# One-hot rows for the token tables: two values side by side in place of six

## The chip, the cores and the metric

The kernel runs on one core of a Trainium2 chip. The metric is the device time of one execution in microseconds; a kernel is given by the median of its runs. The engines are TensorE (matmuls, PE in the profile; its weight loads PEld), VectorE (DVE), ScalarE (ACT), GpSimd (POOL) and SyncE (SP, which issues most DMAs).

## The reference

Three layers follow each other on 4,608 tokens (8 batches of 576) of 512 features:

```python
# 1. attention without a score matrix, per batch and head (8 heads of 64)
q_s = softmax(q, over the head's features); k_s = softmax(k, over the sequence)
x = q_s @ (k_s.T @ v)                       # (4608, 512)
# 2. mixture of 8 experts, the best two for each token
n = x @ w_gate + log1p(exp(x @ w_noise)) * noise
top2 = the two largest of n; weights = softmax(n[top2])
out[t] += weight * relu(x[t] @ w1[e]) @ w2[e]      # for the two experts e of token t
# 3. soft mixture: 32 slots, 4 for each of 8 experts
logits = x @ phi; d = softmax over tokens; c = softmax over slots
y = c @ experts(d.T @ x)                    # (4608, 512)
```

For layer 2 the kernel has to find out, on the chip, which tokens belong to which expert. That list, the table of tokens by expert, is what the change is about.

## The kernel before, in words

**Stages.** Tokens are taken in four pairs of batches, nine tiles of 128 tokens each. The attention of pairs 0 to 2 and part of pair 3 runs first (the string FIRST lists its steps in order); then the experts begin with ten blocks of two tiles of tokens from pairs 0 and 1, and the rest of the attention (the string MIX) is spread over these blocks. Then come blocks of three tiles, blocks of two tiles, all under conditions on the number of blocks, and at the end the soft mixture (the tail).

**The gate of a part of a pair.** `gate(T0, T1)` (L329) runs twice for each pair of batches, on six tiles and on three. It computes noisy logits, ranks the experts, and gives each chosen (token, expert) a place: the place's row `bf` (0 to 127) and column `af` (0 to 287, 36 columns for each of 8 experts). The table `tab` of 128 rows by 288 columns then has to hold the token's number + 1 at that place. It is built by matmuls: for the tile t and choice q of its tokens, `ob` holds in each token's row a one-hot row of 128 values, scaled by the token's number (L419 compares with the constant columns `k.cols`, L420 multiplies with `k.tok1`), and `oa` a one-hot row of 288 values (L427, in `columns`). The matmul of L437 multiplies the two and sums over all tiles and choices in `pa`: twelve matmuls for six tiles, six for three. L442, or L445 to L447, add `pa` to `tab`.

**Layout before.** All are 2-byte floats. `ob` is laid out as [128 partitions, 128 columns, 12 rows], `oa` as [128 partitions, 288 columns, 6 rows]; the constant `k.cols` repeats each number six times (L85). VectorE works on six rows at a time (CW = 6), so neighbouring values in memory are six rows' values of one column, and a matmul that takes one row reads every twelfth value of `ob` (24 bytes apart) as weights and every sixth of `oa` (12 bytes apart) as the moving operand.

**Order.** The steps are emitted in the order of FIRST and MIX; a gate is a generator that goes on at the entries "bg". Within that, a planner orders each engine's instructions by its own costs. Every engine works its queue in order, so that a matmul waiting for VectorE's rows holds up what stands behind it on TensorE.

**Other lines that the prediction's steps name:** L268 and L269 (k.T @ v), L299 and L303 (attention's output), L277 (scaling k.T @ v on VectorE), L744 (splitting weights into two parts, on ScalarE and VectorE), L762 and L764 (transposing and splitting the experts' rows), L777 (experts' first matmul, 256 columns), L807 (their second, 512 columns), L221 (ScalarE's copy of the maxima).

Of the kernel before, what the change touches and what calls it, by code (L numbers as in the profile page):

```python
# [21 lines left out]
P = 128  # L22
B, H, S, DH = 8, 8, 576, 64
D = H * DH
E = 8
# [6 lines left out]
# blocks of two tiles: NPA on the tokens of the first two pairs of batches, up to NPB later, NST of  # L32
# them in any case; in between up to NTR of three tiles
# [3 lines left out]
GT = 6  # L37
# [4 lines left out]
# steps of attention(): of pair i, part j as "stepi.j", a or v behind it: on ScalarE or VectorE.  # L42
# Those before the experts' first blocks,
# [3 lines left out]
# and during those, spread over SPREAD parts  # L47
# [24 lines left out]
def gate_consts(k, ap):  # L72
    nc = k.nc
    # lt[p', p] = 1 where p' < p
# [6 lines left out]
    # columns 0 .. 287, each CW times  # L81
    it = ap.tile([P, E * TE], I32, name="it")
    nc.gpsimd.iota(it, pattern=[[1, E * TE]], base=0, channel_multiplier=0)
    k.cols = ap.tile([P, E * TE, CW], F16, name="cols")
    nc.scalar.copy(k.cols, it.unsqueeze(2).to_broadcast([P, E * TE, CW]))  # L85
# [4 lines left out]
    # local token number + 1 of (p, j), and E * TE * 128 offsets of experts  # L90
# [10 lines left out]
    # tril[e, f] = 1 where f < e  # L101
    k.tril = ap.tile([P, E, E], F32, name="tril")
    nc.gpsimd.affine_select(out=k.tril, in_=k.ones[:, :64].rearrange("p (e f) -> p e f", e=E), pattern=[[1, E], [-1, E]], compare_op=ALU.is_gt, fill=0.0, base=0, channel_multiplier=0)
    # tri[r, e] = 1 where e < r
# [6 lines left out]
def attention(k):  # L111
    """x rows and the dense gates of every token into k.xtab; the tables of tokens by expert. Pauses
    once when the experts can begin, then after every further step."""
    nc, tc = k.nc, k.tc
    with ExitStack() as ctx:
# [5 lines left out]
        # what the experts take the place of  # L121
# [12 lines left out]
        # columns of two heads in KB, each in its own rows: features, parts of the logits, sums  # L134
# [34 lines left out]
        def zero(n):  # L169
            """Part n of x2, first the rows of the first two pairs; and the rows of x that free places read."""  # L170
            z = zz[n % 2]
            if n < 2:
                nc.gpsimd.memset(z, 0.0)
            # not before the rows of x so far
            nc.gpsimd.tensor_copy(z[:, 0:1], after[0][:, 0:1])
            nc.gpsimd.memset(z[:, 0:1], 0.0)
            if n == NZ:
                nc.sync.dma_start(k.xtab[NTOK:, :D], z)
                nc.sync.dma_start(k.xtab[NTOK:, D:], z[:, :E])
            half = k.x2[:NTOK // 2] if n < NZ else k.x2[NTOK // 2:]  # L180
            xr = half.rearrange("(p r) d -> p r d", p=P)
            n_r = half.shape[0] // P
            r = slice(n % NZ * n_r // NZ, (n % NZ + 1) * n_r // NZ)
            nc.sync.dma_start(xr[:, r], bcast(z, 1, r.stop - r.start))
# [14 lines left out]
        # softmax over the sequence: k - max, exp; the sums come with kv  # L199
# [36 lines left out]
        # softmax over the head's features: q - max, exp; the sums come with x  # L236
# [86 lines left out]
        def heads(T0, T1, eng):  # L323
            """Sums of the heads' parts of the logits."""
            lr = lgrs[T0 // TP][:, T0 % TP:T0 % TP + T1 - T0]
            for w in (4, 2, 1):
                eng.tensor_add(lr[:, :, 0:w], lr[:, :, 0:w], lr[:, :, w:2 * w])

        def gate(T0, T1):  # L329
# [14 lines left out]
            # (w - 1) - u, what 1 + u gained  # L344
# [14 lines left out]
            # rank by value, then by number of expert; the first two are taken  # L359
# [14 lines left out]
            # 7 - e + r1 - r2 of the other seven are before it, under 2 for the two  # L374
# [4 lines left out]
            # place of a token among those of its experts  # L379
# [36 lines left out]
            ob = sp.tile([P, P, 2 * GT], F16, name="ob")  # L416
            parts = [slice(m, m + CW) for m in range(0, 2 * n_t, CW)]
            for ms in parts:
                nc.vector.tensor_tensor(ob[:, :, ms], k.cols[:, :P], bcast(flat(bf)[:, ms], 1, P), op=ALU.is_equal)  # L419
                nc.vector.tensor_tensor(ob[:, :, ms], ob[:, :, ms], bcast(flat(k.tok1)[:, ms], 1, P), op=ALU.mult)  # L420
                yield 1
# [3 lines left out]
            def columns(ms):  # L425
                oas.append(sp.tile([P, E * TE, CW], F16, name="oa", bufs=2))
                nc.vector.tensor_tensor(oas[-1], k.cols, bcast(flat(af)[:, ms], 1, E * TE), op=ALU.is_equal)  # L427
# [6 lines left out]
            for ms in parts:  # L434
                oa = oas.pop(0)
                for m in range(ms.start, ms.stop):
                    nc.tensor.matmul(pa, ob[:, :, m], oa[:, :, m - ms.start], start=m == 0, stop=m == 2 * n_t - 1)  # L437
                if len(oas) and ms.stop < 2 * n_t - CW:
                    columns(slice(ms.stop + CW, ms.stop + 2 * CW))
                yield  # L440
# [10 lines left out]
        def back(n):  # L451
            while bg and n:
                try:
                    # 1 marks where only the last pair's pause
                    if next(bg[0]) is None or fine[0]:
                        n -= 1
                except StopIteration:
                    bg.pop(0)
# [72 lines left out]
def table(k):  # L531
    """Tokens of the tables' places; free ones are given rows of their own."""
    nc = k.nc
    m = k.ac.tile([P, E * TE + TE], F32, name="pl_m")
    nc.vector.memset(m[:, E * TE:], 0.0)
    nc.vector.tensor_scalar(m[:, :E * TE], k.tab, 0.0, k.pad1, op0=ALU.is_equal, op1=ALU.mult)
    nc.vector.scalar_tensor_tensor(m[:, :E * TE], k.tab, -1.0, m[:, :E * TE], op0=ALU.add, op1=ALU.add)
    return m
# [10 lines left out]
def block_experts(k, en, n, eoh, eq):  # L549
    """Experts of n blocks, given the experts' first blocks; and where they are the first of theirs."""  # L550
# [8 lines left out]
def block_loads(k, eq, name):  # L559
    """Experts to load for blocks, E for none."""  # L560
# [12 lines left out]
def plan_first(k, cnt):  # L573
    """The first NPA blocks, of two full tiles each, from the first two pairs of batches."""
# [26 lines left out]
    # how many of each expert these are  # L601
# [4 lines left out]
    # rows of the first block  # L606
# [5 lines left out]
def plan(k, cnt):  # L612
    """The other blocks: of three tiles, one for each expert whose number of tiles is odd, and of two
    tiles; their tokens, experts and numbers."""
# [4 lines left out]
    # tiles of each expert, its pairs and threes; running sums of these  # L619
# [13 lines left out]
    # a three takes a pair, if there is one  # L633
# [11 lines left out]
    # where the tables begin, and where they go  # L645
# [14 lines left out]
    for e in range(E):  # L660
        # an even expert's three is written over
# [6 lines left out]
    # behind the last three is the first pair  # L668
# [24 lines left out]
def experts(k, att, rs):  # L693
    """Blocks of tokens through their experts; the steps of `att` go in between in the first ones."""
    nc, tc = k.nc, k.tc
    with ExitStack() as ctx:
# [3 lines left out]
        # banks by use; there are more of them after the attention  # L700
# [8 lines left out]
        # weights by quarters of the hidden features, then rounded and what that left  # L709
# [9 lines left out]
        # rows of x of the next block, its gates, and the present ones  # L719
# [27 lines left out]
        # numbers of blocks: NPA, NPB and one behind them, NTR of three tiles and one behind them  # L747
# [21 lines left out]
        def hidden(b, u):  # L769
            """Part u of the hidden features of a pair, transposed."""  # L770
# [12 lines left out]
        def hidden1(b, u):  # L783
            """The same of a third tile."""
# [24 lines left out]
        def scatter(b, s, py):  # L809
# [4 lines left out]
            # a pair has free places in its second tile only  # L814
# [4 lines left out]
        def block(b, n_s, n, n_n):  # L819
            """Block b of n_s tiles; what the next block n (of n_n tiles) needs runs ahead."""  # L820
# [3 lines left out]
            # a block that may follow several others finds its first weights in the same buffers  # L824
# [45 lines left out]
        for b in range(NPA):  # L870
            if b == NPA - 1:
                # read by all engines, and by none too early
# [33 lines left out]
        # whatever came last has made the first pair ready  # L906
# [18 lines left out]
# buffers of 8 KB for the tail: NA of weights that are loaded while the experts run, NB and 4 others;  # L925
# where rows, further weights and results go
# [4 lines left out]
def tail_weight(k, n, w, after=None):  # L931
    """Weights of the slots' experts in the order in which they are used: four experts at a time,
    a quarter of the inner dimension at a time, two experts in a buffer. Not loaded before `after` is there."""
# [16 lines left out]
def tail(k, rs, rg):  # L950
    nc, tc = k.nc, k.tc
    with ExitStack() as ctx:
# [30 lines left out]
        # st[(g, s), (h, s')] = 1 where s == s'  # L983
# [33 lines left out]
        # softmax over the tokens of part g of the rows, and its share of the slots' inputs, in steps  # L1017
# [65 lines left out]
        def s_s(g):  # L1083
            """The parts' shares, scaled once all maxima are there; their sum."""
# [8 lines left out]
            # the slots' inputs, transposed, but for the sums' reciprocals; those of other experts' slots are zero  # L1093
# [4 lines left out]
        def s_M(g):  # L1098
            """What the parts' shares are scaled by."""
# [13 lines left out]
        def s_Q(g):  # L1113
            """The reciprocals of the sums, by rows (h, s)."""
# [8 lines left out]
        # softmax over the slots  # L1123
# [36 lines left out]
        def c_tr(i):  # L1160
            """The softmax's rows transposed (hi, lo, hi, lo)."""
# [68 lines left out]
        # the slots' experts  # L1230
# [36 lines left out]
        # the slots' outputs (hi, hi, lo, lo)  # L1267
# [42 lines left out]
def _tiles(a):  # L1310
    """(8, 576, c) -> (4, 128, 9, c): pair of batches, partition, tile."""
# [7 lines left out]
def _untile(t):  # L1319
    """(4608, c) in order of tiles -> (4608, c) in order of batches."""  # L1320
# [32 lines left out]
```

## Time and profile before

| | |
|---|---|
| median of 3 runs | 1271.38 us (1265.96 to 1276.61) |
| profiled execution, first to last instruction (span) | 1266.1 us; what lies around the span is not shown |
| TensorE busy | 1169.8 us, 92% of the span |
| VectorE busy | 821.4 us, 65% |
| ScalarE busy | 586.9 us, 46% |
| GpSimd busy | 371.7 us, 29% |
| instructions | 21,319 |
| granted TensorE clock, mean | 0.962 of full |

Busy shares are averages over stages with different limits: the attention ends at about 215 us, the ten blocks and the blocks of three tiles at about 654, the pairs at 1113, then the tail. The duration of a matmul runs from its start to its modelled end and overlaps with the next one's; how long the engine is held is read from one start to the next.

### The profile page before, as it was taken

Reading aid. Unit: us, or ns where it says so; the run is one execution under the profiler, and the core shown is the slowest. Engines: PE = TensorE matmul, PEld = TensorE weight load, DVE = VectorE, ACT = ScalarE, POOL = GpSimd, SP = SyncE. Lnnn points to the kernel's source line nnn. Section 1 sums busy time; section 2 is a strip of 40 time slices with the busy share of each in tenths; the row PEclk is TensorE's granted clock in tenths of the full one; section 3 lists DMA queues with packets and bytes.
Section 4 is the critical chain, followed back from the end, with each engine's and each line's share of the span. In section 5 each row is a group of like instructions: output and inputs, shape, how many; then the busy total and the mean of one; then the engine's idle time right before and its main releaser. Section 6 shows DMA issues by size and latency. Waiting matters only on the chain. (4 is left out here: it accounts for less than half of the span.)

```text
span 1266.1 us, 21319 instructions
## 1 busy us (share of the span) xinstructions
PE 1169.8 (92%) x7792; PEld 1006.6 (80%) x7792; DVE 821.4 (65%) x1468; ACT 586.9 (46%) x887; POOL 371.7 (29%) x397
## 2 busy tenths in 40 slices
PE   4686789999999999999997999999999999987995
PEld 3675667899789889999886989989889899875642
DVE  7988976758686665555554666666666666664753
ACT  3554564556444454444443544544445445433424
POOL 6655643223334222222123223223232122120000
PEclk9877888999999999999998999999999999998998
DMA  9848235467364566665656838365646336128697
GB/s 342 286 149 286 101 115 179 118 200 242 76 167 107 137 172 170 168 167 150 152 161 177 269 84 219 103 204 109 204 100 159 95 72 164 34 47 301 226 377 303
DMA packets 115336, 218.01 MB, mean 172 GB/s; under 512 B 13712, under 2 KB 53776, under 8 KB 111120
## 3 DMA queue, kind: packets, MB, share of 16 engines
q1 hardware_dynamic: 98176, 176.05, 40.7%
q0 software_dynamic: 17040, 40.44, 17.2%
q8 instruction: 65, 1.06, 0.4%
q14 instruction: 55, 0.45, 0.1%
HBM read 243.31 MB, written 48.65 MB: 231 GB/s over the span
## 5 line engine op out<-in xcount | busy, mean ns | idle before, releaser
L744 DVE TENSOR_TENSOR R1l<-ringS,R1h 128x1024 fp32r<-128x1024 f32 x96 | 117.6, 1225 | 101.7 <-ACT R1h L744 98.3
L744 DVE TENSOR_TENSOR R0l<-ringS,R0h 128x1024 fp32r<-128x1024 f32 x95 | 116.4, 1225 | 102.3 <-ACT R0h L744 95.6
L744 DVE TENSOR_TENSOR R2l<-ringS,R2h 128x1024 fp32r<-128x1024 f32 x91 | 111.5, 1225 | 90.3 <-ACT R2h L744 81.1
L744 ACT ACTIVATE R1h<-ringS 128x1024 fp32r<-128x1024 f32 x96 | 101.7, 1060 | 141.5 <-PE py L807 84.1
L744 ACT ACTIVATE R0h<-ringS 128x1024 fp32r<-128x1024 f32 x95 | 100.8, 1062 | 136.6 <-PE py L807 75.9
L744 ACT ACTIVATE R2h<-ringS 128x1024 fp32r<-128x1024 f32 x91 | 96.5, 1060 | 145.6 <-PE py L807 81.8
L777 PE MATMUL ph<-xh,R0h 128*128 128x256 f32 x400 | 112.6, 282 | 1.1 <-DVEq L898 1.0
L777 PE MATMUL ph<-xl,R0h 128*128 128x256 f32 x400 | 112.9, 282 | 0.0
L690 POOL DMA_INDIRECT xg<-xtab,pl_idx x40 | 49.4, 1234 | 214.3 <-DVE sc L767 199.3
L777 PE MATMUL ph<-xh,R0l 128*128 128x256 f32 x400 | 112.2, 280 | 0.0
L781 DVE SCALAR_TENSOR_TENSOR hl<-ph,hh 128x512 fp32r<-128x512 f32 x140 | 95.8, 685 | 24.0 <-ACT hh L780 20.4
L777 PE MATMUL ph<-xh,R2h 128*128 128x256 f32 x360 | 102.5, 285 | 1.9 <-DVE hl L781 1.9
L777 PE MATMUL ph<-xl,R2h 128*128 128x256 f32 x360 | 102.0, 283 | 0.5 <-DVE xl L764 0.5
L777 PE MATMUL ph<-xh,R2l 128*128 128x256 f32 x360 | 101.8, 283 | 0.0
L777 PE MATMUL ph<-xh,R1h 128*128 128x256 f32 x360 | 101.4, 282 | 0.2 <-DVE hl L781 0.2
L813 POOL DMA_INDIRECT x<-y,pl_idx x40 | 63.6, 1589 | 128.9 <-DVE y L812 118.9
L777 PE MATMUL ph<-xl,R1h 128*128 128x256 f32 x360 | 100.6, 279 | 0.0
L777 PE MATMUL ph<-xh,R1l 128*128 128x256 f32 x360 | 100.5, 279 | 0.0
L780 ACT ACTIVATE hh<-ph 128x512 fp32r<-128x512 f32 x140 | 81.8, 584 | 32.5 <-PE ph L777 29.2
L807 PE MATMUL py<-R1l,hh 128*128 128x512 f32 x200 | 80.4, 402 | 0.0
L807 PE MATMUL py<-R1h,hl 128*128 128x512 f32 x200 | 79.3, 398 | 0.0
L777 PEld LDWEIGHTS ph<-xh,R0h 128*128 128x128 f32 x400 | 75.4, 189 | 2.3 <-issue 1.4
(440 smaller groups left out, 3158.9 us busy)
## 6 DMA issues: line engine op xcount, KB each, us to landing
ringS<-in_moe_w_dram SPq DMA_DIRECT2D x292, 512.0 KB
ringA<-in_moe_w_dram SPq DMA_DIRECT2D x12, 1024.0 KB
ringA<-in_moe_w_dram SPq DMA_DIRECT2D x22, 512.0 KB
xtab<-xr SPq DMA_DIRECT2D x36, 256.0 KB
kt<-in_k_dram SPq DMA_DIRECT2D x8, 1024.0 KB
v<-in_v_dram SPq DMA_DIRECT2D x8, 1024.0 KB
x<-z SPq DMA_DIRECT2D x5, 1280.0 KB
ringS<-x SPq DMA_DIRECT2D x5, 1024.0 KB
```

The lines of the kernel that those rows point to most:

```text
L690: k.nc.gpsimd.indirect_dma_start(out=x, out_offset=None, in_=k.xtab[:n], in_offset=bass.IndirectOffsetOnAxis(ap=idx, axis=0))
L744: turn[1:] = [nc.scalar.activation(r[0], f, AF.Copy), nc.vector.tensor_sub(r[1], f, r[0].bitcast(F32))]
L777: nc.tensor.matmul(ph[:, g, :], w[i][:, c, g * P:(g + 1) * P], x[:, c, :], start=n == 0, stop=n == 11)
L780: nc.scalar.activation(hh[:, fs, :], ph, AF.Relu)
L781: nc.vector.scalar_tensor_tensor(hl[:, fs, :], ph, 0.0, hh[:, fs, :].bitcast(F32), op0=ALU.max, op1=ALU.subtract)
L807: nc.tensor.matmul(py[s], a[h], w[i][:, f, :], start=u == 4 and f == n == 0, stop=u == 7 and f == 1 and n == 2)
L813: d = nc.gpsimd.indirect_dma_start(out=k.x2[:NTOK // 2] if b < NPA else k.x2, out_offset=bass.IndirectOffsetOnAxis(ap=at(b, s), axis=0), i ...
```

## The change

`k.cols` repeats each column number twice in place of six times. `ob` is laid out as [128 partitions, tile, 128 columns, 2 choices] and `oa` as [128 partitions, 3 tiles, 288 columns, 2 choices], so that the two choices of one tile's token lie side by side, and a matmul reads every second value (4 bytes apart). VectorE still handles three tiles (six rows) in one instruction; constant columns and the values compared are broadcast to that shape. Comments are taken out elsewhere in the file; that is left out here.

```diff
-    k.cols = ap.tile([P, E * TE, CW], F16, name="cols")
-    nc.scalar.copy(k.cols, it.unsqueeze(2).to_broadcast([P, E * TE, CW]))
+    k.cols = ap.tile([P, E * TE, 2], F16, name="cols")
+    nc.scalar.copy(k.cols, it.unsqueeze(2).to_broadcast([P, E * TE, 2]))
...
-            ob = sp.tile([P, P, 2 * GT], F16, name="ob")
-            parts = [slice(m, m + CW) for m in range(0, 2 * n_t, CW)]
+            ob = sp.tile([P, GT, P, 2], F16, name="ob")
+            parts = [slice(m, m + CW // 2) for m in range(0, n_t, CW // 2)]
+            over = lambda x, ms, n: bcast(x[:, ms], 2, n)
             for ms in parts:
-                nc.vector.tensor_tensor(ob[:, :, ms], k.cols[:, :P], bcast(flat(bf)[:, ms], 1, P), op=ALU.is_equal)
-                nc.vector.tensor_tensor(ob[:, :, ms], ob[:, :, ms], bcast(flat(k.tok1)[:, ms], 1, P), op=ALU.mult)
+                n_p = ms.stop - ms.start
+                nc.vector.tensor_tensor(ob[:, ms], bcast(k.cols[:, :P], 1, n_p), over(bf, ms, P), op=ALU.is_equal)
+                nc.vector.tensor_tensor(ob[:, ms], ob[:, ms], over(k.tok1, ms, P), op=ALU.mult)
                 yield 1
...
             def columns(ms):
-                oas.append(sp.tile([P, E * TE, CW], F16, name="oa", bufs=2))
-                nc.vector.tensor_tensor(oas[-1], k.cols, bcast(flat(af)[:, ms], 1, E * TE), op=ALU.is_equal)
+                n_p = ms.stop - ms.start
+                oas.append(sp.tile([P, CW // 2, E * TE, 2], F16, name="oa", bufs=2)[:, :n_p])
+                nc.vector.tensor_tensor(oas[-1], bcast(k.cols, 1, n_p), over(af, ms, E * TE), op=ALU.is_equal)
...
-                for m in range(ms.start, ms.stop):
-                    nc.tensor.matmul(pa, ob[:, :, m], oa[:, :, m - ms.start], start=m == 0, stop=m == 2 * n_t - 1)
-                if len(oas) and ms.stop < 2 * n_t - CW:
-                    columns(slice(ms.stop + CW, ms.stop + 2 * CW))
+                for m in range(2 * ms.start, 2 * ms.stop):
+                    nc.tensor.matmul(pa, ob[:, m // 2, :, m % 2], oa[:, m // 2 - ms.start, :, m % 2], start=m == 0, stop=m == 2 * n_t - 1)
+                if len(oas) and ms.stop < n_t - CW // 2:
+                    columns(slice(ms.stop + CW // 2, ms.stop + CW))
                 yield
```

## Rows read from the trace of the kernel before

**Rows 1.** Busy us by stage: window, length, PE, PEld, DVE, ACT, POOL, clock, DMA.

```profile
100.00:140.00 40.00, 32.48 (x194) 27.07 (x194) 35.86 (x88) 24.67 (x46) 22.62 (x27) 0.82 0.70 230
...
215.40:654.00 438.60, 435.77 (x2832) 389.87 (x2831) 271.94 (x502) 205.24 (x307) 117.00 (x123) 0.99 0.57 154
...
676.00:1113.00 437.00, 432.46 (x2799) 391.23 (x2800) 276.43 (x390) 209.32 (x257) 117.42 (x103) 0.99 0.52 138
```

**Rows 2.** The tiles ob, oa, cols: count, ns min/median/max, first and last start.

```profile
L437 PEld LDWEIGHTS <-ob x72: 138/145/168, 100.7 to 363.5; 128*128 128x128 f16 x72
L437 PE MATMUL pk<-oa,ob x72: 544/567/587, 100.7 to 363.9; 128*128 128x288 f16 x72
L419 DVE TENSOR_TENSOR ob<-cols,bf x12: 546/557/2699, 93.5 to 353.9; 128x768 f16<-128x768 f16 x12
...
L427 DVE TENSOR_TENSOR oa<-cols,af x12: 1008/1051/1142, 91.5 to 352.9; 128x1728 f16<-128x1728 f16 x12
...
L85 ACT CAST cols<-it x1: 1631/1631/1631, 2.1 to 2.1; 128x1728 f16<-128x1728 int32 x1
```

**Rows 3.** TensorE in order of time: start, us, instructions [idle before <-releaser].

```profile
100.69 4.84 PE L437 MATMUL pk<-oa,ob 128*128 128x288 f16 x12 [7.19 <-DVE ob L420]
...
140.58 2.51 PE L437 MATMUL pk<-oa,ob 128*128 128x288 f16 x6 [1.14 <-DVE ob L420]
...
155.57 1.09 PE L283 MATMUL pt<-ident,KB 128*128 128x128 f32 x4 [4.27 <-DVE KB L277]
...
170.56 4.83 PE L437 MATMUL pk<-oa,ob 128*128 128x288 f16 x12
175.22 2.39 PE L299 MATMUL pv<-KB,qT 128*128 128x162 f32 x16
...
183.19 2.47 PE L437 MATMUL pk<-oa,ob 128*128 128x288 f16 x6
...
210.11 4.80 PE L437 MATMUL pk<-oa,ob 128*128 128x288 f16 x12
...
215.42 0.56 PE L777 MATMUL ph<-xh,R1h 128*128 128x256 f32 x1
...
318.72 4.84 PE L437 MATMUL pk<-oa,ob 128*128 128x288 f16 x12
...
323.79 0.63 PE L807 MATMUL py<-R1h,hl 128*128 128x512 f32 x1
324.22 0.63 PE L807 MATMUL py<-R1l,hh 128*128 128x512 f32 x1
```

**Rows 4.** TensorE in order of time, two neighbours of the experts' first matmul.

```profile
219.08 0.28 PE L777 MATMUL ph<-xh,R2l 128*128 128x256 f32 x1
219.20 0.28 PE L777 MATMUL ph<-xh,R2h 128*128 128x256 f32 x1
```

**Rows 5.** Busy us in short stretches; the clock is the number behind POOL.

```profile
100.70:105.40 4.70, 4.70 (x13) 2.00 (x14) 2.10 (x7) 3.65 (x5) 0.00 (x0) 0.50 1.02 293
...
324.00:325.00 1.00, 1.00 (x3) 0.78 (x3) 1.00 (x5) 0.00 (x0) 0.00 (x0) 0.50 0.00 0
...
326.00:327.00 1.00, 1.00 (x8) 0.86 (x7) 0.00 (x0) 0.21 (x1) 0.79 (x2) 1.00 0.62 236
```

**Rows 6.** VectorE in order of time, around three groups of L437.

```profile
94.61 6.50 DVE L420 TENSOR_TENSOR ob<-ob,tok 128x768 f16<-128x768 f16 x2
...
105.56 0.46 DVE L442 COPY tab<-pk 128x288 f32<-128x288 f32 x1 [2.72 <-PE pk L437]
...
175.43 0.46 DVE L445 TENSOR_SCALAR tt<-pk 128x288 f32<-128x288 f32 x1 [5.24 <-PE pk L437]
...
212.04 0.69 DVE L764 TENSOR_TENSOR xl<-ph,xh 128x512 fp32r<-128x512 f32 x1
```

**Rows 7.** One of the page's costliest groups: busy us, mean ns, idle before it.

```profile
L744 DVE TENSOR_TENSOR R1l<-ringS,R1h 128x1024 fp32r<-128x1024 f32 x96 | 117.6, 1225 | 101.7 <-ACT R1h L744 98.3
```

**Rows 8.** ScalarE in order of time, its first work behind L85.

```profile
12.17 0.59 ACT L221 COPY ms<-pt 128x512 f32<-128x512 f32 x1 [8.43 <-PE pt L219]
```

## The prediction

> **What bounds the kernel now.** I read the busy shares by stage first. TensorE is busy 435.8 of 438.6 us between 215.4 and 654 us and 432.5 of 437 us in the later pairs; from 100 to 140 us VectorE is busy 35.9 of 40 us and TensorE 32.5 [rows 1]. So there are two regimes: up to about 215 us a chain that passes between VectorE and TensorE, from there on TensorE alone. Time taken from TensorE's queue counts in full in the second; in the first it counts where VectorE waits for it.
>
> Second, the lines that the change touches. The 72 matmuls of L437 last 567 ns each, their weight loads 145; the VectorE rows take 557 ns (L419, and L420 alike) and 1,051 ns (L427) [rows 2]. Third, TensorE in order of time: how long the queue is held per matmul is read from start to next start, since durations overlap. The twelve from 170.56 hold it until 175.22 [rows 3]: 4.66/12 = 0.388, written 0.389 below, the rate of the other groups too. There are twelve and six for each of four pairs of batches, 72 in all; the sixes of pairs 2 and 3 repeat the one of 183.19. The weight load of 145 ns fits into 0.389, so the moving operand, 288 columns with 12 bytes from one to the next, sets the rate.
>
> The nearest full-rate row is L777: 256 columns of 4-byte values side by side, one matmul every 0.12 us (219.08 to 219.20) [rows 4]. Scaled to 288 columns that is 0.133 us. At the lower clock L807 takes 0.43 us for 512 columns (323.79 to 324.22) [rows 3], so 288 columns would take 0.24.
>
> Fourth, the clock. [...] The engine had been busy with strided matmuls just before it fell. Fifth, who waits: VectorE stands still 2.72 us before L442 at 105.56 and 5.24 us before L445 at 175.43, both for L437 [rows 6].
>
> **The change, part by part.** *The matmuls.* Columns of both operands come to lie 4 bytes apart. No row shows a matmul of 2-byte values at a 4-byte step. Bounds: 0.389 us (nothing gained, the 12-byte step) and 0.133 (4-byte values at a 4-byte step, the same addresses per column). I take 0.133, as the address step equals that of the second row; the gain is 0.256 us a matmul at the full clock, 0.389 - 0.242 = 0.147 at the half.
> [...] No run here shows the new step yet.
>
> Experts' stage (TensorE bound, everything counts):
> - pair 2, six matmuls: 6 x 0.256 = 1.5 us;
> - pair 3, twelve from 318.72: 12 x 0.256 = 3.1, and the half clock behind them: six L807 start in that stretch, at 0.43 in place of 0.24 (twice 256 columns), 1.1 us;
> - pair 3, six matmuls: 1.5.
> Together 7.2 us, 6.1 if the clock still falls.
>
> Attention stage, group by group:
> - pair 0, twelve from 100.69: the engine starts them after 7.19 us of idling and runs at the half clock, so 12 x 0.147 = 1.8 if it stays low, 3.1 if it rises; VectorE can profit by its 2.72 us of waiting at most. I take 2.2.
> - pair 0, six at 140.58: TensorE gains 0.9 to 1.5 us, but then idles 4.27 us for VectorE's L277 at 155.57 [rows 3]; worth 0.
> - pair 1, twelve at 170.56: VectorE's 5.24 us end earlier; 1.8 to 3.1, I take 2.4.
> - pair 1, six at 183.19: between them and L777 at 215.42 TensorE has only short waits, on copies that follow its own work; 1.5, none if the experts' first rows or weights come last.
> - pair 2, twelve at 210.11: L777 behind them starts at 215.42 although its other input, L764's second xl, is there at 212.73 [rows 6]; 1.8 to 3.1, I take 2.4.
> Together 8.5 us, from 5.3 (the low ends, none for the six) to 10.4 (the high ends).
>
> *VectorE's rows.* The same 36 instructions with the same number of elements; the results lie closed up now, but the broadcast operand has runs of two values in place of six. Before, 768 elements in 557 ns and 1,728 in 1,051 ns differ by 960 elements in 494 ns, 0.51 ns an element. No row has runs of two. Bounds: below, nothing (the element rate is the same, and a gap in the output cost nothing that the slope shows); above, the rate of the 4-byte L744, 1,225 ns for 1,024 elements [rows 7], about 1.04 ns an element: +0.41 us for each of 24 and +0.92 for each of 12, 20.7 us of VectorE, of which pairs 0 and 1 and the twelve of pair 2 (12 x 0.92 x 2/3 + 24 x 0.41 x 2/3 = 13.9 us) lie on the chain before 215 us; the rest is hidden under TensorE, VectorE being 272 of 438.6 us busy there [rows 1]. I take nothing: the runs stay closed 4-byte words.
>
> *The constant.* L85 writes 576 values in place of 1,728; it took 1,631 ns [rows 2], and ScalarE has nothing until 12.17 us behind it [rows 8]. Worth nothing; without that cover it would gain about 1 us. No DMA, wait or queue entry is added or moved by hand. The planner orders VectorE's and TensorE's instructions from its own costs, so neighbours may trade places.
>
> **Sum:** 7.2 + 8.5 = 15.7 us, between 11.4 and 17.6. Set against the profiled execution it gives 1266.1 - 15.7 = 1250.4; that span is 0.1 us above the fastest of the three runs and 5.3 under their median, and what lies around it isn't shown. I forecast a median of such runs, so the sum is taken from the median shown: 1271.4 - 15.7 = **1255.7 us**.
>
> **Rivals.**
> 1. *The columns' step isn't the cause, or 4 bytes are still too far for 2-byte values.* Then the pitch stays near 0.389 and the time near 1271. For it: no row has this step. Against: 288 columns at the half clock would need only 0.24, and the rate is the same 0.39 at either clock, so something other than the array holds it. A halfway case (pitch 0.24) would give about 9 us, 1262. Chance 0.12 with the halfway case.
> 2. *VectorE takes runs of two at the 4-byte rate of 1.04 ns an element.* 15.7 gained, up to 13.9 lost: about 1269 to 1270. [...] Against: runs of six show no cost against the 0.51 ns slope. Chance 0.12.
> [...]
> 3. *A wait takes the place of the time saved (slower).* TensorE's queue is in order. In the first group it stood 7.19 us for L420, two instructions of 0.56 us that took 6.50 us from 94.61 [rows 6] while GpSimd worked. If the planner, with other layouts, puts the short matmuls sooner behind their rows, TensorE and all behind it meet such a wait in other groups. At 7.2 us each it decides from the third on: 3 x 7.2 - 15.7 = +6, about 1277. Against: only this group shows a long one (1.14 us at 140.58). Chance 0.08.
> 4. *The gain is there, but the attention stage gives none of it on*, as inputs or GpSimd become the bound: only 7.2 us, 1264. Against: VectorE's two waits. Chance 0.13.
>
> The forecast (11 to 18 us off) keeps 0.55. Its own range is 1254 to 1260, widened by about 5 us either way for the spread of the runs shown. For 8 in 10 the range reaches to rival 4, the halfway case and most of the spread: **1246 to 1268**. One per cent, 12.7 us, is about what a measurement of this kernel can tell from no change. Faster by more takes a gain above 12.7: most of the forecast's share, 0.48, and 0.04 from a halfway case with lucky spread, 0.52. Within one per cent: the rest of the forecast and most of rivals 1, 2 and 4, 0.41. Slower by more: rival 3 and hardly anything else, 0.07.
>
> **What would show it.** L437's starts 0.13 to 0.15 us apart at a granted clock of 1.00 (0.24 at 0.50); L419, L420 and L427 still at 557 and 1,051 ns (958 and 1,958 would be rival 2); VectorE's waits before L442 and L445 shorter by 2 to 3 us; L777's first start near 207 instead of 215.4; no stretch of 0.50 behind pair 3's twelve; everything from the blocks of three tiles on of the same length, only earlier. The prediction fails if the pitch stays, if VectorE's instructions grow, or if a new wait of TensorE appears before 215 us.

## The result and the profile after

The changed kernel takes **1254.3 us** (median of 4 runs, 1252.5 to 1256.1) against 1270.4 us before (4 runs, the three shown above and one more; 1266.0 to 1276.6): a ratio of 0.986 [0.982, 0.990]. That is 16.1 us less; forecast were 15.7 less and 1255.7 us. The profiled execution took 1253.2 us, its span is 1251.3, so 1.9 us lie around the span; its span is 14.8 us shorter than that of before.

The tiles of the change, in the columns of [rows 2]; the lines have moved (L437 is L441 now, L419 L422, L420 L423, L427 L431), L85 has not:

```profile
L441 PEld LDWEIGHTS <-ob x72: 96/97/151, 100.1 to 347.8; 128*128 128x128 f16 x72
L441 PE MATMUL pk<-oa,ob x72: 287/288/448, 100.1 to 347.9; 128*128 128x288 f16 x72
L422 DVE TENSOR_TENSOR ob<-cols,bf x12: 544/548/6207, 92.7 to 339.3; 128x768 f16<-128x768 f16 x12
L423 DVE TENSOR_TENSOR ob<-ob,tok x12: 541/548/1751, 99.5 to 342.2; 128x768 f16<-128x768 f16 x12
...
L431 DVE TENSOR_TENSOR oa<-cols,af x12: 1005/1050/1056, 90.8 to 338.3; 128x1728 f16<-128x1728 f16 x12
...
L85 ACT CAST cols<-it x1: 671/671/671, 2.1 to 2.1; 128x576 f16<-128x576 int32 x1
```

The matmul lasts half as long (288 ns for 567); VectorE's rows have not moved (548 and 1,050 ns for 557 and 1,051). Over the whole span TensorE has 18.3 us less to do (1151.5 for 1169.8). By the pitches below, 60 matmuls that are 0.26 us shorter and 12 that are 0.15 shorter make 17.4 of it; the rest, 0.9 us, is about what other matmuls save that no longer run at the half clock (six at 0.24 in place of 0.43 us are 1.1):

```profile
PE 1151.5 (92%) x7792; PEld 1001.5 (80%) x7792; DVE 821.3 (66%) x1468; ACT 585.5 (47%) x887; POOL 371.0 (30%) x397
```

TensorE in order of time, as in [rows 3]; the experts' first matmul, L777 before, is L781, their second, L807, is L811:

```profile
100.12 3.06 PE L441 MATMUL pk<-oa,ob 128*128 128x288 f16 x12 [7.88 <-DVE ob L423]
102.97 2.19 PE L299 MATMUL pv<-KB,qT 128*128 128x162 f32 x8
...
138.10 0.94 PE L441 MATMUL pk<-oa,ob 128*128 128x288 f16 x6 [0.51 <-DVE ob L423]
...
153.05 1.09 PE L283 MATMUL pt<-ident,KB 128*128 128x128 f32 x4 [6.53 <-DVE KB L277]
...
168.01 2.49 PE L441 MATMUL pk<-oa,ob 128*128 128x288 f16 x12
170.34 2.37 PE L299 MATMUL pv<-KB,qT 128*128 128x162 f32 x16
...
178.28 0.92 PE L441 MATMUL pk<-oa,ob 128*128 128x288 f16 x6
180.01 1.32 PE L303 MATMUL pv<-KB,qT 128*64 128x162 f32 x16 [0.81 <-ACT xr L315]
...
204.52 1.70 PE L441 MATMUL pk<-oa,ob 128*128 128x288 f16 x12
206.05 0.60 PE L256 MATMUL pt<-ident,qt 128*128 128x128 f32 x4
206.53 0.39 PE L781 MATMUL ph<-xh,R1h 128*128 128x256 f32 x1
207.21 0.39 PE L781 MATMUL ph<-xl,R1h 128*128 128x256 f32 x1 [0.29 <-DVE xl L768]
...
308.36 1.70 PE L441 MATMUL pk<-oa,ob 128*128 128x288 f16 x12
309.80 0.49 PE L811 MATMUL py<-R1l,hh 128*128 128x512 f32 x1
...
347.28 0.94 PE L441 MATMUL pk<-oa,ob 128*128 128x288 f16 x6
347.96 0.38 PE L781 MATMUL ph<-xh,R1h 128*128 128x256 f32 x1
```

Twelve matmuls at the full clock now last 1.70 us from the first start to the last end. Less the last one's 0.288 and over eleven steps that is a pitch (the time from one start to the next) of 0.128 us; at the half clock (100.12) it is (3.06 - 0.448)/11 = 0.237.

The clock, in the columns of [rows 5], and the experts' stage, in those of [rows 1]:

```profile
206.50:640.00 433.50, 430.22 (x2841) 388.79 (x2840) 275.08 (x511) 205.36 (x308) 117.92 (x125) 1.00 0.57 156
100.12:102.97 2.85, 2.85 (x12) 1.80 (x13) 2.10 (x7) 2.16 (x4) 0.00 (x0) 0.50 1.00 287
309.80:312.80 3.00, 3.00 (x18) 2.52 (x16) 2.13 (x7) 0.60 (x1) 1.30 (x2) 1.00 0.64 212
206.05:206.70 0.65, 0.65 (x7) 0.54 (x5) 0.65 (x4) 0.00 (x0) 0.00 (x0) 1.00 0.00 0
```

The first group still runs at 0.50. Behind the twelve of pair 3 the clock now stays at 1.00, where it was 0.50 [rows 5]. TensorE is as full as before in the experts' stage (430.2 of 433.5 us). The last row is the stretch behind the twelve of pair 2. In the kernel before, the same stretch, and the six of 183.19 with what follows it, show:

```profile
214.80:215.50 0.70, 0.70 (x6) 0.70 (x4) 0.55 (x2) 0.00 (x0) 0.00 (x0) 0.50 0.00 0
183.20:185.50 2.30, 2.30 (x8) 0.70 (x5) 2.03 (x14) 2.28 (x10) 0.60 (x2) 1.00 0.11 42
185.60:187.60 2.00, 2.00 (x23) 1.77 (x23) 2.00 (x12) 1.00 (x3) 0.00 (x0) 1.00 0.70 262
```

VectorE in order of time, for [rows 6] (L442 is L446, L445 is L449):

```profile
92.73 6.68 DVE L422 TENSOR_TENSOR ob<-cols,bf 128x768 f16<-128x768 f16 x2
...
103.21 0.46 DVE L446 COPY tab<-pk 128x288 f32<-128x288 f32 x1 [0.95 <-PE pk L441]
...
170.54 0.46 DVE L449 TENSOR_SCALAR tt<-pk 128x288 f32<-128x288 f32 x1 [2.90 <-PE pk L441]
```

Its two waits have lost 1.77 and 2.34 us.

**Where the time came from.** The lead of the new kernel over the old one, at the same instruction of both traces, in us:

| instruction (before, after) | lead | step |
|---|---|---|
| first twelve (100.69, 100.12) | 0.6 | 0.6, not from the matmuls |
| L299 behind it (105.35, 102.97) | 2.4 | +1.8 |
| L283 behind pair 0's six (155.57, 153.05) | 2.5 | +0.1 |
| L299 behind pair 1's twelve (175.22, 170.34) | 4.9 | +2.4 |
| behind pair 1's six (185.59, 180.01) | 5.6 | +0.7 |
| experts' first matmul (215.42, 206.53) | 8.9 | +3.3 |
| behind pair 2's six (252.15, 241.80) | 10.4 | +1.5 |
| behind pair 3's twelve (326.50, 311.87) | 14.6 | +4.3 |
| behind pair 3's six (364.38, 348.17) | 16.2 | +1.6 |
| end of the pairs' blocks, the start of the DMA x<-y,pl_idx on the chain that ends last (1113.19, 1097.30) | 15.9 | -0.3 |
| end (1266.1, 1251.3) | 14.8 | -1.1 |

The 0.6 us ahead of the first group is no gain of the change: two other executions of the same changed kernel (after_again and after_5, below) start that group at 102.38 and 100.50. The last 1.1 us are given back in the tail, which has none of the changed work, and are no effect of the change either: from the DMA to the end it takes 154.0 us here and 152.9 before, but 152.9 and 153.6 in those two executions. In them the experts' first matmul starts at 206.82 and 205.61, and the lead at the end of the pairs' blocks is 15.4 and 17.3. So the total lead is good to 1 or 2 us, and the single steps are those of one pair of traces.

### The profile page after: what moved, and what is told of

It reads as the page before. It is cut to its first block, busy times and chain, and to the rows that moved or that the text cites. A ratio compares the mean times of both kernels' runs of the same rounds, so it can differ in the third digit from the quotient of the medians.

```text
span 1251.3 us, 21319 instructions
## 1 busy us (share of the span) xinstructions
PE 1151.5 (92%) x7792; PEld 1001.5 (80%) x7792; DVE 821.3 (66%) x1468; ACT 585.5 (47%) x887; POOL 371.0 (30%) x397
## 5 line engine op out<-in xcount | busy, mean ns | idle before, releaser
L781 PE MATMUL ph<-xh,R0h 128*128 128x256 f32 x400 | 112.6, 282 | 1.1 <-DVEq L902 1.0
L781 PE MATMUL ph<-xl,R0h 128*128 128x256 f32 x400 | 112.6, 282 | 0.0
L781 PE MATMUL ph<-xh,R0l 128*128 128x256 f32 x400 | 112.2, 280 | 0.0
L781 PE MATMUL ph<-xh,R2h 128*128 128x256 f32 x360 | 102.2, 284 | 1.9 <-DVE hl L785 1.9
L781 PE MATMUL ph<-xl,R2h 128*128 128x256 f32 x360 | 102.0, 283 | 0.5 <-DVE xl L768 0.5
L781 PE MATMUL ph<-xh,R2l 128*128 128x256 f32 x360 | 101.8, 283 | 0.0
L781 PE MATMUL ph<-xh,R1h 128*128 128x256 f32 x360 | 100.8, 280 | 0.2 <-DVE hl L785 0.2
L781 PE MATMUL ph<-xl,R1h 128*128 128x256 f32 x360 | 100.4, 279 | 0.3 <-DVE xl L768 0.3
L781 PE MATMUL ph<-xh,R1l 128*128 128x256 f32 x360 | 100.3, 279 | 0.0
L811 PE MATMUL py<-R1l,hh 128*128 128x512 f32 x200 | 79.5, 398 | 0.0
L811 PE MATMUL py<-R1h,hl 128*128 128x512 f32 x200 | 78.8, 396 | 0.0
L781 PEld LDWEIGHTS ph<-xh,R0h 128*128 128x128 f32 x400 | 75.4, 189 | 2.3 <-issue 1.4
```

What stands on the lines that cost most here:

```text
L781: nc.tensor.matmul(ph[:, g, :], w[i][:, c, g * P:(g + 1) * P], x[:, c, :], start=n == 0, stop=n == 11)
L811: nc.tensor.matmul(py[s], a[h], w[i][:, f, :], start=u == 4 and f == n == 0, stop=u == 7 and f == 1 and n == 2)
```

## The experiments

Theory: the moving operand's step sets the matmul's pitch, and all of the gain comes from `oa`. Rivals: `ob`'s step counts too; the attention stage passes nothing on; VectorE pays for its shape. Each kernel is compared with the kernel before on the same chip; edits are against the changed kernel, with lines left out at "...". moving_only, weights_only and late_only also get a second constant that repeats each number six times, for the old half; ScalarE writes it behind L85, in an instruction of the shape of the old L85 (1.63 us in the kernel before), ahead of its other work.

**moving_only** keeps the old `ob` and has the new `oa`.

```diff
-            ob = sp.tile([P, GT, P, 2], F16, name="ob")
+            ob = sp.tile([P, P, 2 * GT], F16, name="ob")
...
-    nc.tensor.matmul(pa, ob[:, m // 2, :, m % 2], oa[:, m // 2 - ms.start, :, m % 2], ...)
+    nc.tensor.matmul(pa, ob[:, :, m], oa[:, m // 2 - ms.start, :, m % 2], ...)
```

> Only the moving operand oa has the new layout (4 bytes from column to column); the weights ob stay 24 bytes apart. Theory (the moving operand's step sets the rate): matmul starts 0.13 to 0.15 us apart at the full clock, the whole gain, 1254 to 1256 us against 1270 before. Rival (the weights' step holds it too): starts 0.25 us apart or more, 1260 or above.

Measured: 1257.8 us, ratio 0.988 [0.981, 0.994], span 1254.5. The tile ob in its trace:

```profile
L444 PEld LDWEIGHTS <-ob x72: 138/143/169, 102.3 to 349.1; 128*128 128x128 f16 x72
L444 PE MATMUL pk<-oa,ob x72: 287/295/459, 102.3 to 349.2; 128*128 128x288 f16 x72
```

Its twelve of pair 3, and the clock behind them:

```profile
309.49 1.80 PE L444 MATMUL pk<-oa,ob 128*128 128x288 f16 x12
```

```profile
311.00:314.00 3.00, 3.00 (x18) 2.52 (x17) 2.11 (x6) 0.60 (x1) 1.21 (x2) 1.00 0.62 197
```

The weight loads are the long ones of before, and the matmuls are short all the same. The loads do show a little: the pitch is (1.80 - 0.295)/11 = 0.137 us for 0.128 in the changed kernel, at loads of 143 ns, which are now longer than the time from one matmul's start to the next. That is 0.6 us over 72 matmuls, which the times can't tell from nothing.

**weights_only** is the other half: the new `ob`, the old `oa`.

```diff
-    oas.append(sp.tile([P, CW // 2, E * TE, 2], F16, name="oa", bufs=2)[:, :n_p])
+    oas.append(sp.tile([P, E * TE, CW], F16, name="oa", bufs=2))
...
-    nc.tensor.matmul(pa, ob[:, m // 2, :, m % 2], oa[:, m // 2 - ms.start, :, m % 2], ...)
+    nc.tensor.matmul(pa, ob[:, m // 2, :, m % 2], oa[:, :, m - 2 * ms.start], ...)
```

> Only the weights ob have the new layout; the moving operand oa stays 12 bytes from column to column. Theory: starts 0.39 us apart as before, weight loads 97 ns in place of 145, and no gain: 1268 to 1272 us. Rival (the weights' step sets the rate): 1254 to 1258.

Measured: 1271.9 us, ratio 1.001 [0.998, 1.004], span 1269.9. Its tile ob, and a stretch behind pair 3's twelve:

```profile
L444 PEld LDWEIGHTS <-ob x72: 96/118/152, 104.6 to 366.9; 128*128 128x128 f16 x72
L444 PE MATMUL pk<-oa,ob x72: 539/562/568, 104.6 to 367.3; 128*128 128x288 f16 x72
```

```profile
327.00:328.00 1.00, 1.00 (x4) 0.77 (x3) 1.00 (x5) 0.00 (x0) 0.00 (x0) 0.50 0.00 0
```

Shorter weight loads are worth nothing beside the slow matmuls (118 ns in the median, against 562 for the matmul). The two halves together show that the gain is `oa`'s, and that the half clock behind pair 3's twelve comes and goes with the slow matmuls (0.50 here, 1.00 in moving_only).

**late_only** has the new layout for pairs 2 and 3 alone (`new = T0 >= 2 * TP`, and the old shapes and matmul where it is false).

> The new layout for the gates of pairs 2 and 3 only; pairs 0 and 1 keep the old one. Theory (what the attention stage gains is passed on to the end): 1.8 + 2.3 + 0.7 = 4.8 us of the changed kernel's gain are lost, 1259 us, and the experts' first matmul starts at about 211 us. Rival (the attention stage's gain is another thing, such as the moment at which the clock rises, and is there anyway): 1254 to 1256, first matmul near 207.

Measured: 1258.4 us, ratio 0.987 [0.982, 0.993], span 1256.4, 5.1 us over that of the changed kernel. Its TensorE at the end of the attention (the experts' first matmul is L797 here):

```profile
209.84 2.17 PE L457 MATMUL pk<-oa,ob 128*128 128x288 f16 x12
...
212.19 0.37 PE L797 MATMUL ph<-xh,R1h 128*128 128x256 f32 x1
```

It reaches the experts 5.7 us after the changed kernel (5.4 and 6.6 after its two other executions) and 3.2 before the old one, so what pairs 0 and 1 save does reach the experts, and nearly all of it the end of the span. The medians stand 4.1 us apart, 2.6 from after_5 on the same chip, with overlapping ranges, so this reading rests on the traces, three of the changed kernel and one of late_only.

**flat_rows** puts the columns side by side (a step of 2 bytes). VectorE's broadcast operand then repeats a single value along the innermost axis, and with it goes the run of two.

```diff
-            ob = sp.tile([P, GT, P, 2], F16, name="ob")
+            ob = sp.tile([P, 2 * GT, P], F16, name="ob")
+            one = lambda x, rs, n: bcast(flat(x)[:, rs], 2, n)
...
-    oas.append(sp.tile([P, CW // 2, E * TE, 2], F16, name="oa", bufs=2)[:, :n_p])
-    nc.vector.tensor_tensor(oas[-1], bcast(k.cols, 1, n_p), over(af, ms, E * TE), op=ALU.is_equal)
+    oas.append(sp.tile([P, CW, E * TE], F16, name="oa", bufs=2))
+    nc.vector.tensor_tensor(oas[-1], bcast(k.cols, 1, 2 * n_p), one(af, rs, E * TE), op=ALU.is_equal)
```

> One-hot rows with the columns side by side (2 bytes apart), so that VectorE's broadcast operand repeats one value in its innermost run. Theory: matmuls no faster than in the changed kernel (0.13 us apart), VectorE's instructions at one element a cycle (958 and 1,958 ns), of which up to 13.9 us lie on the chain before the experts: about 1268 us. Rival (VectorE is covered there): not over 1259. Third: VectorE keeps 550 and 1,050 ns and the time is that of the changed kernel, 1254.

Measured: 1282.0 us, ratio 1.008 [1.004, 1.012], span 1279.3: slower than the kernel before, and 14 us over what was expected. The tiles, then VectorE and TensorE in time:

```profile
L444 PEld LDWEIGHTS <-ob x72: 95/98/152, 105.9 to 365.6; 128*128 128x128 f16 x72
...
L424 DVE TENSOR_TENSOR ob<-cols,bf x12: 895/947/2036, 102.2 to 357.3; 128x768 f16<-128x768 f16 x12
...
L434 DVE TENSOR_TENSOR oa<-cols,af x12: 1943/1952/7611, 92.8 to 355.5; 128x1728 f16<-128x1728 f16 x12
```

```profile
92.85 9.48 DVE L434 TENSOR_TENSOR oa<-cols,af 128x1728 f16<-128x1728 f16 x2
```

```profile
226.83 0.36 PE L784 MATMUL ph<-xh,R1h 128*128 128x256 f32 x1
...
336.99 1.64 PE L444 MATMUL pk<-oa,ob 128*128 128x288 f16 x12
```

The matmuls are as fast as at 4 bytes ((1.64 - 0.286)/11 = 0.123 us), so closing the step wholly gives next to nothing. VectorE takes 947 and 1,952 ns, about twice the time, one element in 1.05 ns ((1,952 - 947)/960) for 0.52 with the run of two. (The expectation's "one element a cycle" is 958 and 1,958 ns worked out from the 1.04 ns an element of L744 [rows 7]; how long a cycle of VectorE lasts no run shows.) The two L434 lost another 5.6 us (9.48 for 2 x 1.95) while GpSimd was at work (94.32 to 100.5). The experts begin 20.3 us later than in the changed kernel, where 13.9 were counted, and pair 3's twelve start 28.6 us later (336.99 against 308.36). The sum left out such standing and the waits that TensorE then has: its L444 matmuls wait 15.9 us for L425's rows, in five places, for 8.4 in two in the changed kernel. The order of the steps is another one too (pair 2's twelve now stand behind the experts' first matmul, from 227.46 on), and how much of the 28 us that accounts for was not separated.
Between these two layouts lie 548 ns with the run of two and 947 with the repeated value, for 768 elements; why the repeated value costs that much no run shows.

**step8** and **step16** keep all of the change but `oa`, whose columns lie 8 and 16 bytes apart. In step8 VectorE takes four rows in an instruction, in step16 six of eight places.

```diff
-NZ, CW = 4, 6
+NZ, CW = 4, 4                       # step8 alone
...
+    oas.append(sp.tile([P, E * TE, 4], F16, name="oa", bufs=2))    # step16: 8 in place of 4
+    o = oas[-1][:, :, 0:2 * n_p].rearrange("p c (t q) -> p c t q", q=2)
+    nc.vector.tensor_tensor(o, bcast(k.cols, 2, n_p), bcast(af[:, ms], 1, E * TE), op=ALU.is_equal)
```

> The moving operand with 8 bytes from column to column (rows of two tiles side by side in fours); the weights as in the changed kernel. VectorE writes oa in five instructions for each pair of batches in place of three. [...] Rival (the rate falls in proportion to the step): 0.24 to 0.26 us apart, 1260 to 1264.

> The moving operand with 16 bytes from column to column (rows of six in places for eight); the weights as in the changed kernel. [...] Rival (any step past 8 bytes costs the same): 0.39 us, 1268 to 1272.

Measured: step8 1269.5 us, ratio 0.998 [0.995, 1.001]; step16 1279.8 us, ratio 1.006 [1.003, 1.010]. A six of step8, with the L813 on either side of it 0.24 us apart as at a clock of 1.00 (0.43 at 0.50), and a twelve of step16, behind which the clock was 0.50 (340 to 343 us):

```profile
322.60 1.70 PE L443 MATMUL pk<-oa,ob 128*128 128x288 f16 x6
```

```profile
334.36 6.26 PE L443 MATMUL pk<-oa,ob 128*128 128x288 f16 x12
```

Their matmuls last 0.436 and 0.687 us in the median; with that taken off for the last one the pitch is (1.70 - 0.436)/5 = 0.253 and (6.26 - 0.687)/11 = 0.507 us; a six of step16 (196.77, 3.21 us) gives 0.505. That 8 bytes would cost no more than 4 (0.13 us apart, 1255 to 1258 us) had been expected, and fell; the rival, that the time goes with the distance, holds from 4 bytes on. For step16 0.389 x 4/3 = 0.52 us and 1276 to 1280 us had been expected, and came; its rival (0.39) fell. The pitches by step:

| step | pitch, us (288 columns) | bytes passed per ns |
|---|---|---|
| 2 bytes (flat_rows) | 0.123 | 4.7 |
| 4 (after) | 0.128 | 9.0 |
| 8 (step8) | 0.253 | 9.1 |
| 12 (before) | 0.388 | 8.9 |
| 16 (step16) | 0.507 | 9.1 |

step16's time lies about where its pitch puts it: 72 x (0.507 - 0.388) = 8.6 us more of TensorE than before, and 6.9 us in the medians (1279.8 against 1272.9). step8's lies above both ranges that were expected (1255 to 1258 and 1260 to 1264 us) and does not decide anything: with more and smaller VectorE instructions (20 for `oa` in place of 12, 752 ns in the median) the attention ran in another order, and the experts began at 221.85 us, later than in the kernel before or after. What that cost was not separated, so for step8 the pitch alone is read.

**after_again** and **ks_vector** ran side by side. The first is the changed kernel once more; the second also moves the subtraction of two steps (ks2.0 and ks3.0 in FIRST) from GpSimd to VectorE, so that GpSimd is idle while the first group's rows are made.

```diff
-qm2.1 ks2.0 kv1.1 ... qm3.0 ks3.0 bg
+qm2.1 ks2.0v kv1.1 ... qm3.0 ks3.0v bg
```

> The changed kernel itself, for comparison on the same chip: 1252 to 1257 us.

> The changed kernel, with the subtractions of k's maxima of the first batches of pairs 2 and 3 on VectorE in place of GpSimd. Theory (the 7.9 us for which TensorE stands before the first group come from VectorE's one-hot rows standing about 5.7 us while GpSimd works on k): VectorE does those 3.1 us of work itself and stands no longer, 2 to 5 us off for both places together, 1249 to 1252. Rival (VectorE is the bound there, and 2 x 3.1 us more work is as long as the standing was): 1253 to 1258.

Measured: after_again 1254.4 us, ratio 0.987 [0.981, 0.993]; ks_vector 1250.6 us, ratio 0.982 [0.977, 0.987]. ks_vector's TensorE at the first group, and its VectorE ahead of it:

```profile
96.92 3.06 PE L441 MATMUL pk<-oa,ob 128*128 128x288 f16 x12 [2.70 <-DVE ob L423]
```

```profile
95.19 1.02 DVE L422 TENSOR_TENSOR ob<-cols,bf 128x768 f16<-128x768 f16 x2
```

The same two L422 take 1.02 us in place of 6.68, and TensorE's wait falls from 7.88 to 2.70: VectorE did stand for GpSimd. Only some of it arrives: the experts begin at 205.07, 1.5 us sooner. Part is lost again at pair 1's twelve, whose first half now waits 4.47 us for L423 (165.20), where the changed kernel has no wait and after_again 1.34 (for the second half).

**ks_vector_5** and **after_5** are those two again, with more runs each, to settle whether that is worth anything.

> The same as ks_vector, in more rounds, for an interval against the changed kernel beside it: 2 to 5 us under it if the standing behind GpSimd was the cost, no less than 1 us under it otherwise.

> The changed kernel itself in more rounds on the same chip: 1252 to 1257 us, 14 to 18 us under the kernel before.

(Where the first says "no less than 1 us under it otherwise", at most 1 us is meant.) Measured: 1251.4 us, ratio 0.985 [0.981, 0.988], and 1255.8 us, ratio 0.988 [0.984, 0.991]. The median is about 4 us lower both times, and of all pairings of a run of one with a run of the other, ks_vector is the lower in 15 of 16 and 29 of 36. Yet the intervals overlap, and the two profiled spans are 1250.0 and 1249.5 us. That ks_vector beats the changed kernel is likely, but not settled.

## Why the prediction was right

**The pitch.** 0.133 us was taken from a row of 4-byte values at the same step, 0.24 for the half clock; 0.128 and 0.237 were measured. The choice of that end of the bounds was right, and the table of steps shows why: up to 4 bytes the step costs next to nothing, from there on the pitch goes with it. The reason given, that the address step counts and not the size of a value, fits, but no run has 4-byte values at a wider step, so it isn't shown. Rival 1 fell; its halfway case is the pitch of an 8-byte step (0.253 us).

**The experts' stage.** Pair 2's six were put at 1.5 us, pair 3's twelve with the half clock behind them at 4.2, its six at 1.5: 7.2 in all, and 1.5, 4.3 and 1.6 came, with TensorE as full as before. That the half clock (0.50 from 324 to 325 us, 1.00 from 326 [rows 5]) would go with the slow matmuls was a guess with a price on either side (7.2 or 6.1); weights_only keeps the half clock (0.50) and moving_only does not (1.00).

**The attention.** 8.5 us were forecast and 8.9 came, but the parts differ:
- pair 0's twelve: 1.8 for 2.2. The clock did not rise within the group, which is the low end;
- pair 0's six: 0.1 for 0. TensorE was done earlier and then idled 6.53 us for L277 in place of 4.27 [rows 3];
- pair 1's twelve: 2.4 for 2.4, VectorE's wait 2.34 shorter [rows 6];
- pair 1's six: 0.7 for 1.5. Behind them TensorE now waits 0.81 us for ScalarE's xr (L315), where it had no wait before;
- pair 2's twelve: 3.3 for 2.4. The pitch gave its high end, 12 x 0.26 = 3.1. The clock behind this group was 0.50 before as well (214.8 to 215.5) and is 1.00 now (206.05 to 206.7), which the sum had only for pair 3;
- the rest is the 0.6 us ahead of the first group.

So the errors of single terms, 0.4 to 0.9 us, cancelled; that the total agrees better than its parts is luck. Rival 4 (nothing passed on) fell by the lead at the experts' first matmul and by late_only.

**VectorE and the constant.** Taken at nothing, and the rows have the same durations (548 and 1,050 ns for 557 and 1,051). That the closed words of 4 bytes keep them so is the author's reason; no run tests it alone. (The upper bound of 20.7 us is 24 x 0.41 + 12 x 0.92 = 20.9; nothing rests on it.) Rival 2 did not happen, but flat_rows, whose VectorE rows take what that rival gave them (1.05 ns an element), suggests that its price was undersized: 1,269 to 1,270 us were given for it, and 1,282 came, slower than the kernel before. VectorE's own time was not all that was lost there, though its order of steps differs as well. L85 is 0.96 us shorter at 2.1 us, in the cover of [rows 8].

**Rival 3**, waits of 7 us each in other groups, did not come. One such wait stays in the first group (7.88 us for 7.19), with its stretched instruction now L422 in place of L420; ks_vector shows its cause. A new wait of TensorE before 215 us was also one of the signs by which the prediction was to fail. There are two, of 0.81 and 0.29 us (and one of 1.34 and 1.47 at pair 1's twelve in the two other executions); they took back part of single terms and not the sum.

**The total.** 16.2 us of lead behind the last changed matmul, 0.6 of it from elsewhere, leave 15.6 for a sum of 15.7. In the spans 14.8 remain, in the medians 16.1; the runs of one kernel spread by more than that difference.

## What to carry to other kernels

Look at how many bytes lie between neighbouring columns of a matmul's moving operand: with 2-byte values the engine passed about 9 bytes a ns in each partition here (8.9 to 9.1 at steps of 4 to 16 bytes), a 4-byte step cost next to nothing (0.128 us for 0.123 at 2 bytes), and every further doubling, to 8 and 16 bytes, doubled the pitch (0.253 and 0.507 us). A layout that both engines can take lies in between: pairs side by side kept VectorE at 0.52 ns an element and TensorE at 0.128 us a matmul, where six cost TensorE three times the pitch (0.388) and one cost VectorE twice the time (1.05 ns an element). The step of the weights mattered little: loads of 145 ns cost nothing beside matmuls 0.39 us apart, and 143 ns raised a pitch of 0.128 us to 0.137.

## What the runs showed of the hardware that was not expected

- The pitch of the 12-byte step did not depend on the granted clock: 0.388 us in the first group at 0.50 [rows 3, 5], and (2.47 - 0.567)/5 = 0.381 in the six of 183.19 at 1.00. That of the 4-byte step did: 0.237 and 0.128.
- Twelve slow strided matmuls in a row were followed by a lower clock, with TensorE counted as busy all through them (4.78 us of 318.72 to 323.50): 0.50 behind the twelve of pairs 2 and 3 in the kernel before and of pair 3 in weights_only and step16 (340 to 343 us), 1.00 behind that of pair 3 in the changed kernel and moving_only. Six of them were not (1.00 behind the six of 183.19), nor were the twelve of 170.56, in which the clock rose (0.81 in the mean; 1.00 from 175.2 to 177). What decides it no run tried.
- Two VectorE instructions of 0.55 us each took 6.68 us while GpSimd worked on its own tensors (92.74 to 98.99), and 1.02 us when it did not. The second of them lasted 6.21 us: it ended only behind three GpSimd instructions in a row.
- Weight loads at a 24-byte step took 145 ns, at a 4-byte step 97 (118 beside the slow matmuls of weights_only); a 24-byte step thus cost the weights far less (1.5 times) than the 12-byte step cost the moving operand (0.388 us for 0.128, three times).
